# A written-out instruction order, its first part put in another order

## The chip, the cores and the metric

The kernel runs on one core of a Trainium2 chip. The metric is the device time of one execution in microseconds (us). The core has five engines with an instruction stream each: PE (matmuls, into the eight banks of PSUM), ACT (activations, copies out of PSUM, and it can issue DMAs), DVE (vector work), POOL (vector work without PSUM) and SP (which only issues DMAs here). Each stream is executed in its own order; between streams there are semaphores.

## The reference

A transformer block: layer norm, attention with a compressive memory, residual, layer norm, a feed-forward layer with SiLU, residual. 2048 tokens, width 640, 32 heads of 20, four segments of 512 tokens, feed-forward width 1728, bf16.

```python
for s in range(N):                      # N = 4 segments of L = 512 tokens
    logits = einsum(qs, ks) * scale + mask
    p = softmax(logits); a_dot = einsum(p, vs)
    pq = phi(qs)                        # phi(t) = t + 1 if t > 0 else exp(t)
    a_mem = einsum(pq, M) / (einsum(pq, z) + 1e-06)
    outs.append(g * a_mem + (1.0 - g) * a_dot)
    pk = phi(ks)
    M = M + einsum(pk, vs); z = z + einsum(pk)
h = x + concat(outs) @ wo
out = h + silu(layernorm(h) @ w1) @ w2
```

## The kernel before

The work is written as some 1430 tasks with a name each. Functions declare them segment by segment: `declare_front` (layer norm, q and k projections, V, gather copies), `declare_memory`, `declare_ticks` (attention of one group of four heads) and `declare_back` (output projection, second layer norm, feed-forward layer, output). A long string, `ORDER`, then says in which order the tasks are emitted; a word in it is `name/engine:slots`, so `vt05/S:0` is the task `vt05`, issued by SP (A is ACT, D is DVE, G is POOL), with slot 0 of the rotating buffer that it is the first to use. `schedule` reads the words in turn, checks that producers stand ahead and that a slot is free, and appends each task's instructions to the stream of its engine. So the string alone sets each engine's order, the engine of a task that may run on two, and the PSUM banks; there is no timing in it. A `Tracker` adds the semaphore waits that the order needs: a task that writes a PSUM bank waits for the instruction that last read it.

```python
t = todo.pop(name)
t.eng = {"A": AC, "D": DV, "G": PO, "S": SP}[eng] if eng else list(t.engs)[0]
for a in t.allocs:
    if a.slot is None:
        a.slot = slots.pop(0)
```

The tasks of segment 0 that matter here, with their lines and names in `ORDER`:

- projections of q and k by halves of 256 tokens (L867, `pr...x`, `pr...y`) and their evictions from PSUM to SBUF on ACT (L883) or DVE (L884), `qe...`; segment 1 has them whole, 512 tokens wide. `re_wq`, `re_wk` rearrange the weights for them (L693 on ACT, L695 on DVE).
- gather copies (L915, `vt0...`): twelve DMAs that bring rows of q and k of heads 20 to 31 into a layout of their own. They read QK and write QKV; in segment 0 both lie inside the tensor of w2, so that they read w_sb<-w_sb in the trace. The scores of the second four head groups wait for all twelve.
- V projections (L828, `v00` to `v03`, segment 1 `v10` to `v13`), 128 tokens each, and their evictions (L842 on ACT, L843 on DVE, `ve...`).
- scores (L965, `qk...`): four heads at once into four PSUM banks. Then the exp on ACT (L977, `e...`), over two banks (1024 columns) or four (2048), and the causal mask on POOL (L988, `mk...`).
- exponentials of q and k for phi (L890 on ACT, `ex...`), finished on DVE (L897, L903, `pha`, `phb`).
- transposes by DMA: of the normalized tokens of segment 1 (L799, `n1_tr`), of the attention output (L1265, `ot`), of phi(K) (L1208, `kt`). The output projection follows (L1273, `wo0`, `wo1`).
- the feed-forward layer: tanh on ACT (L1317, `th...`), and loads of w1 and w2 (L582, `w_w1_...`, `w_w2_...`). `zf0` and `lsc0` are small exponentials of beta (L649, L638).

Of the kernel before, what the change touches and what calls it, by code (L numbers as in the profile page):

```python
# [324 lines left out]
D = 640  # L325
# [31 lines left out]
epsg0:0 vpad0 zpad w2z/G:0 fill30:7 x0:0 w_q1:0 warm iota mt mta mtb mm7 x1:4 mm0 n1_st1/A:0,0 w_q0 w_q2 epsc sel  # L357
halfc n1_st0/D:5 n1_r0/G n1_r1/D n1_ap0:0 n1_tp0:4 n1_te0a/A:0 n1_ap1:1 n1_tp1:0 n1_te0b/A n1_te1b/D n1_te1a/A w_k0
re_wq1/D:0 pr010x:4 re_wq4/A re_wq2/D pr020x:2 qe020x/A:0 qe010x/A:0 re_wq3/D re_wq0/D pr000x:5 pr040x:6 w_k1
re_wk2/A:0 qe000x/A:0 re_wk1/D qe040x/A:0 pr011x:0 qe011x/A re_wk0/D pr001x:2 pr021x:5 qe001x/A qe021x/A x2:10,5  # L360
n1_st2/D:3 n1_r2/G qk0x10:0 pr030x:7 w_wv0:0 w_wv1 n1_st3/D:1 n1_r3/G e0x10:4 x4:2,1,11,3 qe030x/A:0 w_wo:0 beta
w_w1_0:0 e0x12 re_wk3/D pr031x:6 n1_ap2:2 re_wk4/D x8/S:6,7,8,9 n1_ap3:0 n1_tp2:0 n1_te2/D n1_st6:4 n1_tp3:4 n1_r6/G
n1_te3/A qe031x/D pr041x:7 qe041x/D qk0x20:0 e0x2+:6 pr030y:4 qe030y/D pr031y:5 qe031y/A pr041y:6 qe041y/A pr040y:7
qe040y/A vt02/S:0 vt011/S vt05/S vt08/S n1_st5:1 qk0x30:0 vt04/S mk0x1_0 mk0x1_256 n1_st4:5 n1_r5/G n1_ap5:1 e0x3+:0
n1_ap6:2 pr000y:4 qe000y/D lsc0 vt07/A pr021y:6 qe021y/D pr001y:5 qe001y/D pr011y:7 ex021:0 qe011y/D pr020y:1 n1_r4/D
# [12 lines left out]
h1_0_7_0:6 e6ya+:0 th0_7_0:0 s0_7_0:0 h1_0_12_0:0 th0_12_0:1 qk7ya0:1 e7ya+:1 kt01:0 w_w2_5 h1_0_4_0:7 tn2y:5 s0_12_0
h1_0_3_0:6 kg01/G mk4y1_256 n1_st10:1 th0_3_0:0 mk4y1_384 qvz h1_0_6_0:0 qk4y20:1 th0_4_0:1 nm2y:3 s0_4_0 mm4
h1_0_5_0:5 e4y2+:3 s0_3_0 pr110:7 qe110/D:0 th0_5_0:1 qk4y30:1 pr140:6 th0_6_0:0 e4y32:6 mk4y2_0 e4y30 w_w2_1/S  # L380
mk4y2_256 s0_6_0 s0_5_0 mk4y3_0 mk4y3_256 qe140/D av4y:0 kt03:1 kg03/D ex120:1 qk8a0:4 e8a0:2 e8a2 pr111:1 h1_0_1_0:2
th0_1_0:1 oe4y/D:0 h1_0_8_0:3 th0_8_0:0 qe111/D vt10/S:0 qk8e0:4 s0_1_0 n1_ap8:3 e8e0:4 s0_8_0 mz01:0 ma01/D:3,1
mk4y3_384 av6y:1 e8e2 zf1 qk8b0:2 e8b+:5 kh03/D oe6y/D:1 h1_0_10_0:0 th0_10_0:0 tn4y:6 mzc6 n1_ap9:0 mk8e_0 nm4y:2
tn6y:7 kt04:1 mk8a_0 phb120 nm6y:0 ex100:2 pr130:1 qe130/D:0 qk9a0:3 e9a+:0 s0_10_0 kg04/D pr131:2 qe131/D mk8b_0
pha131:0 h1_0_2_0:7 w_w2_2/S kh04/D th0_2_0:1 mm5 h1_0_11_0:1 th0_11_0:0 s0_11_0 qk9b0:2 e9b0:1 s0_2_0 h1_0_0_0:0
mz02:6 pha101:1 vt13/S mk8b_384 th0_0_0:0 e9b2 mk9a_0 mk9b_0 mk8e_256 h1_0_9_0:7 th0_9_0:1 s0_0_0 ma02/D:0,4,6,7
qk10a0:0 e10a0:3 mzc2 h1_0_13_0:6 h2_0_0:4 e10a2 w_w2_4 ot3 h2_0_1 mk9b_384 mk10a_0 phb101 n1_r10/D pha111:2 vt19/S
mzc0 mb00:0,0 w_w2_3/S s0_9_0 n1_ap11:2 pha100:0 phb100 th0_13_0:0 s0_13_0 ex131:0 phb131 pha110:0 n1_ap10:1 vt12/S
qk10b0:0 e10b+:6 epsg1 av8:7 oe8/D:0 n1_tr8:0 av9:6 oe9/D:1 n1_tr9 ex110:0 phb110 vt18/S vt110/S h2_0_2 mk10b_0
# [1037 lines left out]
```

## Time and profile before

| | |
|---|---|
| three runs | 296.9, 296.9 and 297.67 us, median 296.9 |
| span of the profiled execution | 296.3 us, 0.6 below the median |
| granted PE clock | 1.000 in every stage |
| busy over the span | PE 95%, DVE 75%, ACT 73%, POOL 47% |

The runs are not matched one by one to the profile; the profiled execution's own time is its span and what lies around it, and the 0.6 us between the span and the median is read as that. A timeline row gives start, duration, engine (ACTq and SPq are DMA issues of these engines), line, operation, output and input, and a count where neighbours of one kind are merged; in square brackets stands the idle time before it and what ended that. Consecutive ACT instructions overlap by about 0.1 us in the trace.

### The profile page before, as it was taken

What the parts mean: (1) busy time and instruction counts of PE and PEld (TensorE: products, weight loads), DVE (VectorE), ACT (ScalarE), POOL (GpSimd) and SP (SyncE); (2) the same over time, 40 slices, a digit from 0 to 9 for tenths busy, and PEclk for the clock granted to TensorE, in tenths of its full rate; (3) what the DMA queues carried; (4) which work ended last, traced back from release to release, by engine and by line L of the source; (5) the groups of instructions that cost most, each with busy time, mean ns of one, the idle gap of its engine ahead of it and who ended that gap; (6) DMA issues with size and microseconds to landing.
All of it is one profiled execution on the core that took longest, in us unless ns stands there. A gap on an engine that the chain in (4) does not pass through costs nothing.

```text
span 296.3 us, 7415 instructions
## 1 busy us (share of the span) xinstructions
PE 282.1 (95%) x2968; PEld 167.6 (57%) x2991; DVE 222.2 (75%) x506; ACT 217.3 (73%) x266; POOL 140.0 (47%) x257
## 2 busy tenths in 40 slices
PE   7897889999999999999999999999999999999997
PEld 5675445555665455566643545465665457764575
DVE  3897799778979779899698967759967688626522
ACT  4884989999999899998879999788759750014400
POOL 6237735645566477646526646455476620200000
PEclk9999999999999999999999999999999999999999
DMA  7956973803953221255433400144171023220002
GB/s 243 367 173 105 173 133 71 221 18 75 189 94 74 53 60 22 40 109 106 104 96 61 66 1 2 27 76 87 22 99 32 0 61 74 68 67 25 22 22 91
DMA packets 49922, 25.40 MB, mean 86 GB/s; under 512 B 39504, under 2 KB 48048, under 8 KB 49888
## 3 DMA queue, kind: packets, MB, share of 16 engines
q1 hardware_dynamic: 47804, 22.69, 36.2%
q10 hardware_dynamic: 2084, 2.23, 2.4%
q8 instruction: 24, 0.39, 0.5%
q14 instruction: 10, 0.08, 0.1%
HBM read 10.41 MB, written 2.62 MB: 44 GB/s over the span
## 4 chain that ended last, share of the span: by engine, by line
PE 78%; DVE 8%; DMA 6%; issue 2%; ACT 2%; SPq 1%; POOL 1%; DVEq 0%; ACTq 0%
PE ps_all L1350 19%; PE ps_all L1308 17%; PE ps_all L867 12%; PE ps_all L965 7%; PE ps_all L1273 6%; PE ps_all L828 5%; PE ps_all L1009 5%; DMA x_tok<-in_A_x_dram 3%; DMA xT<-xn_rot 2%; ACT PT L977 2%; PE ps_all L1039 1%; DVE stt L743 1%; PE ps_all L1093 1%; DMA w_sb<-w_sb 1%; PE ps_all L1226 1%
## 5 line engine op out<-in xcount | busy, mean ns | idle before, releaser
L977 ACT ACTIVATE PT<-ps_all 128x1024 bf16<-128x1024 f32 (+1 forms) x120 | 153.2, 1310 | 16.9 <-PE ps_all L965 15.7
L988 POOL TENSOR_SCALAR_AFFINE_SELECT PT<-PT 128x512 bf16<-128x512 bf16 x128 | 81.6, 648 | 59.2 <-ACT PT L977 56.9
L1350 PE MATMUL ps_all<-w_sb,sT 128*128 128x320 bf16 (+2 forms) x462 | 64.9, 295 | 0.0
L1308 PE MATMUL ps_all<-hT,w_sb 128*128 128x512 bf16 (+1 forms) x315 | 61.0, 336 | 1.2 <-issue 0.6
L1317 ACT ACTIVATE th<-ps_all 128x512 f32<-128x512 f32 (+2 forms) x70 | 34.1, 505 | 35.3 <-PE ps_all L1308 31.2
L1350 PEld LDWEIGHTS ps_all<-w_sb,sT 128*128 128x128 bf16 x462 | 43.2, 98 | 18.3 <-issue 1.8
L1323 DVE SCALAR_TENSOR_TENSOR sT<-th,ps_all 128x512 bf16<-128x512 f32 (+2 forms) x70 | 37.9, 561 | 17.8 <-ACT th L1317 16.9
L1308 PEld LDWEIGHTS ps_all<-hT,w_sb 128*128 128x128 bf16 x325 | 29.9, 98 | 25.3 <-issue 3.5
L764 POOL TENSOR_TENSOR rst<-rst,eps_c 128x1 f32<-128x1 f32 x32 | 18.3, 576 | 24.4 <-DVE rst L758 23.1
L743 DVE BATCH_NORM_STATS2 stt<-x_tok 128x6 f32<-128x320 bf16 x62 | 27.2, 481 | 1.1 <-DMA x_tok<-in_A_x_dram 0.7
L1363 DVE SCALAR_TENSOR_TENSOR x_tok<-ps_all,x_tok 128x640 bf16<-128x640 f32 (+3 forms) x18 | 13.3, 745 | 16.7 <-PE ps_all L1350 16.6
L1071 POOL TENSOR_TENSOR otok<-on 128x320 bf16<-128x320 bf16 x24 | 19.0, 797 | 11.7 <-DVE on L1063 11.7
L1273 PE MATMUL ps_all<-wo_sb,oT 128*128 128x320 bf16 x160 | 23.8, 299 | 0.0
L884 DVE CAST QK<-ps_all 128x512 bf16<-128x512 f32 x23 | 15.7, 688 | 9.1 <-PE ps_all L867 8.9
L1063 DVE TENSOR_TENSOR on<-ps_all,rd 128x640 bf16<-128x640 f32 x24 | 19.8, 824 | 0.9
L828 PE MATMUL ps_all<-wv_sb,xT 128*128 128x320 bf16 x120 | 18.3, 299 | 1.1 <-DMA xT<-xn_rot 0.9
L1273 PEld LDWEIGHTS ps_all<-wo_sb,oT 128*128 128x128 bf16 x160 | 15.0, 98 | 7.2 <-issue 1.8
L867 PE MATMUL ps_all<-xT,wkr 128*128 128x512 bf16 x67 | 16.9, 379 | 1.2 <-issue 0.8
L867 PE MATMUL ps_all<-xT,wqr 128*128 128x512 bf16 x70 | 17.3, 380 | 0.4 <-issue 0.2
L1009 PE MATMUL ps_all<-PT,Vx 128*32 128x512 bf16 (+3 forms) x384 | 16.4, 301 | 0.1
L843 DVE CAST Vx<-ps_all 128x640 bf16<-128x640 f32 x15 | 12.3, 818 | 5.4 <-PE ps_all L828 5.3
L770 DVE TENSOR_SCALAR xn_rot<-x_tok,mvt,rst 128x640 bf16<-128x640 bf16 x32 | 14.9, 475 | 1.7 <-POOL rst L764 1.0
(106 smaller groups left out, 337.4 us busy)
## 6 DMA issues: line engine op xcount, KB each, us to landing
w_sb<-in_B_w_dram SPq DMA_DIRECT2D x5, 432.0 KB, 6.3
w_sb<-in_B_w_dram SPq DMA_DIRECT2D x3, 480.0 KB, 4.6
x_tok<-in_A_x_dram SPq DMA_DIRECT2D x2, 640.0 KB, 9.7
out_dram<-x_tok ACTq DMA_DIRECT2D x8, 160.0 KB, 1.8
out_dram<-x_tok SPq DMA_DIRECT2D x7, 160.0 KB, 1.9
x_tok<-in_A_x_dram SPq DMA_DIRECT2D x3, 320.0 KB, 3.4
QKV<-QK SPq DMA_DIRECT2D x12, 72.0 KB
wo_sb<-in_A_wo_dram SPq DMA_DIRECT2D x1, 800.0 KB, 10.4
```

What stands on the lines that cost most here:

```text
L743: T.add(DV, lambda e, hh=hh: e.bn_stats(out=stt[:, s, 6 * hh:6 * hh + 6], in_=xb[:, 320 * hh:320 * hh + 320]), reads=R((xa, xsub)), writes ...
L828: fns.append(lambda e, c=c, hh=hh: e.matmul(bank(ps, hh)[:, 0:320], lhsT=xT_[:, c, 128 * i:128 * i + 128], rhs=wv_sb[:, c, 320 * hh:320 * ...
L867: fns = [lambda e, kc=kc: e.matmul(bank(ps)[:, lo:hi], lhsT=wt[:, kc, c, :], rhs=xT_[:, kc, lo:hi], start=(kc == 0), stop=(kc == NC - 1)) ...
L965: fns.append(lambda e, j=j, o=o, r=r, q0=q0, q1=q1, qa=qa, ka=ka: e.matmul(ps_all[:, o:o + q1 - q0], lhsT=ka[32 * r:32 * r + DH, 128 * j:1 ...
L977: T.add(AC, lambda e: e.activation(out=pt[:, pta.slot, q0:q0 + nq, 0:width], in_=sc3[:, b0:b0 + nq, 0:width], func=ACT.Exp, scale=SCALE), ...
L988: T.add(PO, lambda e: e.affine_select(out=v, in_=v, pattern=[[0, 4], [1, 128]], compare_op=ALU.is_ge, fill=0.0, base=0, channel_multiplier ...
L1009: fns.append(lambda e, j=j, r=r, h=h, pa=pa, pt=pt, co=co, q0=q0, ji=ji: e.matmul(bank(po)[32 * r:32 * r + 32, q0:hi], lhsT=Vx[:, vx.slot, ...
L1273: fns.append(lambda e, c=c, hh=hh: e.matmul(bank(ps, hh)[:, 0:320], lhsT=oT[:, c, 128 * i:128 * i + 128], rhs=wo_sb[:, c, 320 * hh:320 * h ...
L1308: fns = [lambda e, c=c: e.matmul(bank(ps)[:, lo:hi], lhsT=w1_sb[:, c, 128 * f:128 * f + 128], rhs=hT[:, c, lo:hi], start=(c == 0), stop=(c ...
L1317: T.add(AC, lambda e: e.activation(out=th[:, tha.slot, lo:hi], in_=bank(ps)[:, lo:hi], func=ACT.Tanh, scale=0.5), reads=R((ps, [0])), writ ...
L1323: T.add(DV, lambda e: e.scalar_tensor_tensor(out=sT[:, f, lo:hi], in0=th[:, tha.slot, lo:hi], scalar=1.0, in1=bank(ps)[:, lo:hi], op0=ALU. ...
L1350: fns.append(lambda e, f=f, t0=t0, fr=fr, hh=hh, n=n: e.matmul(bank(pa, hh)[:, 0:n], lhsT=sT[:, f, t0:t0 + 128], rhs=w2_sb[:, fr, c0 + 320 ...
```

## The change

Only `ORDER` changes. Of the 1426 words no task is added or removed. Up to about word 447 of 1426 the order, the engines of 28 tasks and the slots are new; after that the sequence of names is the old one, with other numbers for some rotating buffers. Two lines of the diff:

```diff
-re_wq1/D:0 pr010x:4 re_wq4/A re_wq2/D pr020x:2 qe020x/A:0 qe010x/A:0 re_wq3/D re_wq0/D pr000x:5 pr040x:6 w_k1
+w_k1 x2:0,1 re_wq4/A:0 re_wq1/D pr010x:7 qe010x/A:0 re_wq0/D re_wq3/D re_wq2/D re_wk1/A:0 re_wk0/D pr000x:1 pr040x:2
...
```

On ACT the place is between the last four-bank exp of the first score groups and the first one of the second (19 to 29 us before). L977 are exps, L915 gather copies, L890 exponentials for phi, L883 evictions of projections, L842 a V eviction, L638 the small exponential. Before:

```order
L977 ACTIVATE PT<-ps_all 128x2048
L638 ACTIVATE bsel<-beta_bc 128x32
L915 DMA w2_sb<-w2_sb 8x2x1024
L890 ACTIVATE ex<-w2_sb 128x512
L915 DMA w2_sb<-w2_sb 8x2x1024
L915 DMA w2_sb<-w2_sb 12x3x1024 x2
L890 ACTIVATE ex<-w2_sb 128x512
L977 ACTIVATE PT<-ps_all 128x1024 x2
```

After:

```order
L977 ACTIVATE PT<-ps_all 128x2048
L915 DMA w2_sb<-w2_sb 8x2x1024 x2
L883 ACTIVATE w2_sb<-ps_all 128x256 x2
L890 ACTIVATE ex<-w2_sb 128x512
L883 ACTIVATE w2_sb<-ps_all 128x256
L915 DMA w2_sb<-w2_sb 8x1x1024
L883 ACTIVATE w2_sb<-ps_all 128x256
L915 DMA w2_sb<-w2_sb 12x3x1024 x2
L890 ACTIVATE ex<-w2_sb 128x512
L915 DMA w2_sb<-w2_sb 8x2x1024
L977 ACTIVATE PT<-ps_all 128x1024
L842 ACTIVATE Vx<-ps_all 128x32x20
```

ACT now issues six gather copies, four of them behind or between evictions that came from DVE, and it also evicts one V block.

On PE the place is the same stretch: V projections (L828) and scores (L965, twelve matmuls in two rows for a group of three blocks, eight for a group of two). Before:

```order
L828 MATMUL ps_all<-wv_sb,hT 128x320 x20
L965 MATMUL ps_all<-w2_sb 128x256 x4
L965 MATMUL ps_all<-w2_sb 128x128 x8
L828 MATMUL ps_all<-wv_sb,hT 128x320 x10
L965 MATMUL ps_all<-w2_sb 128x256 x4
L965 MATMUL ps_all<-w2_sb 128x128 x8
L828 MATMUL ps_all<-wv_sb,hT 128x320 x10
```

After:

```order
L828 MATMUL ps_all<-wv_sb,hT 128x320 x20
L965 MATMUL ps_all<-w2_sb 128x256 x4
L965 MATMUL ps_all<-w2_sb 128x128 x8
L828 MATMUL ps_all<-wv_sb,hT 128x320 x20
L965 MATMUL ps_all<-w2_sb 128x256 x4
L965 MATMUL ps_all<-w2_sb 128x128 x8
L965 MATMUL ps_all<-w2_sb 128x256 x8
```

The fourth V projection now stands ahead of the first scores that need the gather copies, and the next score group directly behind those.

On ACT again, the stretch from the first tanh instructions (L1317) to the exp from which ACT's order is the old one (58 to 66 us before). Before:

```order
L1317 ACTIVATE th<-ps_all 128x256 x2
L977 ACTIVATE PT<-ps_all 128x2048
L1317 ACTIVATE th<-ps_all 128x256 x2
L977 ACTIVATE PT<-ps_all 128x1024 x2
L890 ACTIVATE ex<-QK 128x512
```

After:

```order
L1317 ACTIVATE th<-ps_all 128x256 x2
L977 ACTIVATE PT<-ps_all 128x2048
L1317 ACTIVATE th<-ps_all 128x256 x2
L649 ACTIVATE zf<-beta_bc 128x32
L977 ACTIVATE PT<-ps_all 128x1024
L582 DMA w2_sb<-in_B_w2_dram 128x3x640
L977 ACTIVATE PT<-ps_all 128x1024
L890 ACTIVATE ex<-QK 128x512 x2
L582 DMA w2_sb<-in_B_w2_dram 128x4x640
```

The small exponential, one exponential for phi and two loads of w2 (SP's before) now stand here.

On SP two transposes of phi(K) (`kt00`, `kt02`) and the w1 load `w_w1_2` move from ahead of the transposes of the attention output to behind them; the load `w_w1_1` moves to behind the last transpose of segment 1's tokens (`n1_tr7`), and `w_w1_3` alone is still ahead of it. On PE the output projections `wo1` and `wo0` move from between the score groups `qk3ya` and `qk4ya` to behind `qk4ya` and ahead of `qk3ya`, and the products for the memory (L1226, `mz00`) from their place at 37 us to one at about 54 us of the old timeline.

More of the change, by code (lines that the diff above doesn't have):

```diff
@@ L361 @@
[L361 to L365, printed above, removed]
@@ new lines @@
+vt10/S:0 kg01/G mz01:0 ma01/D:1,2 qk8e0:4 s0_1_0 mm2 e8e0:5 s0_8_0 mk4y3_384 mm6 av6y:1 n1_ap8:3 e8e2 n1_r9/G zf1
+qk8b0:2 e8b+:4 oe6y/D:1 h1_0_10_0:0 tn4y:6 th0_10_0:0 mzc6 n1_ap9:2 mk8e_0 nm4y:0 tn6y:7 kt04:1 mk8a_0 phb120 nm6y:3
+qvz ex100:0 pr130:1 qe130/D:0 qk9a0:3 e9a+:6 s0_10_0 kg04/D pr131:2 mm4 qe131/D mk8b_0 kh03/D pha131:2 kg03/D
+h1_0_2_0:7 w_w2_2/S kh04/D th0_2_0:1 mm5 h1_0_11_0:1 th0_11_0:0 s0_11_0 qk9b0:2 e9b0:3 s0_2_0 h1_0_0_0:0 mz02:6
+pha101:0 vt13/S mk8b_384 th0_0_0:0 e9b2 mk9a_0 mk9b_0 mk8e_256 h1_0_9_0:7 th0_9_0:1 s0_0_0 ma02/D:3,5,4,7 qk10a0:0
@@ new lines @@
+h1_0_11_1:5 th0_11_1:1 vt29/S pha231:0 phb231 phb211 e17b0 wo6:6 mk16e_256 s0_13_1 s0_11_1 qk18b0:2 e18b2:5 mk17b_0
+e18b0 mk18b_0 rs6 n2_st6:1 ex220:0 av16:0 oe16/D:1 wo7:6 rs7 n2_r6/D qk17a0:2 wo4:0 vt28/S e17a+:6 h1_0_9_1:7
+th0_9_1:0 ex240:2 kg10/G vt27/S n2_st7:4 mk18b_384 vt21/S mk17b_384 vt211/S h1_0_3_1:6 mk17a_0 rs4 th0_3_1:1 n2_st4:7
+s0_9_1 qk18e0:2 e18e0:0 n2_r4/D wo5:0 s0_3_1 vt23/S h1_0_2_1:7 e18e2 mk18e_0 phb240 rs5 th0_2_1:0 s0_2_1 h1_0_1_1:6
+th0_1_1:1 vt24/S s0_1_1 qk18a0:2 e18a0:2 vt25/S av17:1 oe17/A:0 kt23:0 x12/S h2_2_0:6 h2_2_1 n2_ap6:0 n2_st5:2
@@ new lines @@
+th1_7_0:1 th1_4_0:0 s1_7_0 s1_4_0 qk20a0:0 e20a+:6 out3/S x14/S n1_st12:2 n1_r12/G h1_1_1_0:4 th1_1_0:1 s1_1_0 vp210/S
+h1_1_12_0:7 th1_12_0:0 mk20b_0 n1_st13:4 n1_r13/G mk20b_384 vp28/S qk20e0:0 h1_1_11_0:5 n1_ap12:3 e20e+:2 h1_1_8_0:4
+qk21a0:0 s1_12_0 th1_11_0:1 h1_1_5_0:6 e21a+:0 th1_5_0:0 n1_st15:6 mk21a_0 n1_ap13:1 mk20a_0 s1_11_0 s1_5_0 mk20e_0
+mk20e_256 h1_1_2_0:7 th1_2_0:1 s1_2_0 vp20/S qk22a0:0 e22a0:3 kt20:1 vp211/S kg20/G:0 n1_st14:3 vp26/S th1_8_0:1
+kg23/D n1_r14/D h1_1_6_0:5 th1_6_0:0 vp29/S n1_tr12:0 v30:6 n1_r15/D s1_6_0 e22a2 h1_1_0_0:0 n1_ap14:2 s1_8_0
@@ L448 @@
[L448 to L449 removed]
+h2_8_0:0 s2_5_0 th2_9_0:0 s2_11_0 th2_8_0:1 s2_8_0 out4/A wo12:2 ot14 h2_8_1 s2_9_0 wo14:6 rs12 n2_st12:6 rs14
+n2_r12/D n2_st14:5 ot13 wo13:2 rs13 n2_st13:4 ot15 n2_r13/G wo15:6 n2_r14/D rs15 n2_st15:3 h2_8_2 h2_8_3 h2_9_1 o8
+out8/S n2_ap13:2 n2_tr13:0 h2_11_0:2 n2_r15/G n2_ap15:0 h2_11_1 n2_tr15 n2_ap12:1 h2_10_0:6 h2_11_2 h2_10_1 n2_ap14:3
```

149 lines of the change are left out of this document (68 added, 81 removed).

## Prediction

> **What bounds the kernel now.** I read the page's first part, then the windows by stage, then the timelines of ACT, PE and SP in the first 66 us, since the orders differ only there.
>
> ```profile
> PE 282.1 (95%) x2968; PEld 167.6 (57%) x2991; DVE 222.2 (75%) x506; ACT 217.3 (73%) x266; POOL 140.0 (47%) x257
> ```
>
> Over the span PE is the fullest. The stages say more (columns: PE, PEld, DVE, ACT, POOL busy, clock, DMA):
>
> ```profile
> 20.00:30.00 10.00, 8.50 (x86) 6.19 (x84) 8.22 (x20) 5.40 (x7) 5.69 (x11) 1.00 0.53 93
> 30.00:40.00 10.00, 8.49 (x156) 4.80 (x155) 8.28 (x18) 9.30 (x10) 8.10 (x14) 1.00 1.05 181
> 40.00:50.00 10.00, 8.99 (x112) 5.33 (x113) 9.57 (x26) 8.77 (x10) 4.47 (x10) 1.00 0.35 84
> 50.00:56.40 6.40, 5.99 (x87) 2.91 (x82) 5.49 (x14) 6.32 (x9) 3.00 (x5) 1.00 0.79 189
> 56.40:66.00 9.60, 9.10 (x111) 5.33 (x112) 6.83 (x18) 9.56 (x13) 5.35 (x9) 1.00 0.25 66
> 66.00:80.00 14.00, 13.47 (x178) 8.58 (x180) 12.23 (x33) 13.85 (x21) 7.38 (x14) 1.00 0.65 126
> 80.00:90.00 10.00, 10.00 (x119) 6.05 (x118) 8.08 (x20) 9.51 (x10) 6.85 (x15) 1.00 0.55 101
> ```
>
> From 50 to 80 us ACT is busy 29.7 of 30.0 us: scores on PE wait for a PSUM bank that an exp on ACT has to empty, so ACT sets the pace there and PE has 0.5 us of idle time in each 10. Between 20 and 50 us neither engine is full; these holes are what an order can win. From 80 us PE is full. On ACT the two lists are the same from this exp on, on PE from a little later:
>
> ```profile
> 66.03 1.94 ACT L977 ACTIVATE PT<-ps_all 128x1024 bf16<-128x1024 f32 x2
> ```
>
> The waits from there on are the same too, but for a few on work that is long done. So the change can only shift the instant at which ACT and PE enter the common part; that shift is the forecast. I follow ACT from mark to mark:
>
> ```profile
> 18.28 0.93 ACT L883 ACTIVATE w_sb<-ps_all 128x256 bf16<-128x256 f32 x3
> 19.12 1.88 ACT L977 ACTIVATE PT<-ps_all 128x2048 bf16<-128x2048 f32 x1
> 19.24 1.62 ACTq L915 DMA_DIRECT2D w_sb<-w_sb  x1
> ...
> 21.36 0.63 ACT L890 ACTIVATE ex<-w_sb 128x512 bf16<-128x512 bf16 x1 [0.24 <-DVE w_sb L884]
> 21.36 3.34 ACTq L915 DMA_DIRECT2D w_sb<-w_sb  x3
> 24.75 0.63 ACT L890 ACTIVATE ex<-w_sb 128x512 bf16<-128x512 bf16 x1 [2.76 <-DVE Vx L843]
> 25.56 1.94 ACT L977 ACTIVATE PT<-ps_all 128x1024 bf16<-128x1024 f32 x2 [0.18 <-PE ps_all L965]
> 28.92 1.88 ACT L977 ACTIVATE PT<-ps_all 128x2048 bf16<-128x2048 f32 x1 [1.43 <-PE ps_all L965]
> 31.30 1.88 ACT L977 ACTIVATE PT<-ps_all 128x2048 bf16<-128x2048 f32 x1 [0.50 <-PE ps_all L965]
> 33.07 0.62 ACT L890 ACTIVATE ex<-w_sb 128x512 bf16<-128x512 bf16 x1
> 33.68 3.71 ACT L977 ACTIVATE PT<-ps_all 128x1024 bf16<-128x1024 f32 x3
> ```
>
> ```profile
> 28.47 0.40 PE L965 MATMUL ps_all<-w_sb 20*128 20x256 bf16 x12 [1.50 <-DMA w_sb<-w_sb]
> 28.80 1.53 PE L828 MATMUL ps_all<-wv_sb,hT 128*128 128x320 bf16 x10
> ...
> 37.00 0.48 PE L1226 MATMUL ps_all<-Vx,phiKt 128*128 128x84 bf16 x8
> ...
> 42.68 1.53 PE L828 MATMUL ps_all<-wv_sb,xT 128*128 128x320 bf16 x10 [0.85 <-DMA xT<-xn_rot]
> 44.48 2.89 PE L1273 MATMUL ps_all<-wo_sb,oT 128*128 128x320 bf16 x20
> ```
>
> Mark A is ACT's exp at 28.92: it follows the scores at 28.47, for which PE stood 1.50 us until the twelve gather copies (L915) had landed. Mark B is 33.68.
>
> **The change part by part.** Up to 18.28 us projections and weight rearrangements trade places, and one rearrangement of wk goes from DVE to ACT.
>
> ```profile
> 10.01 0.66 ACT L883 ACTIVATE w_sb<-ps_all 128x256 bf16<-128x256 f32 x2 [0.72 <-PE ps_all L867]
> 10.56 0.83 ACT L693 ACTIVATE wkr<-sT 128x400 bf16<-128x400 bf16 x2
> ```
>
> One more costs ACT 0.83; the hole of 0.72 covers most of it, and one eviction (0.31) goes the other way while another comes. I take 0.1 us later at the exp that ends the stretch; ends 0 and 0.8 (the hole not used).
>
> *Gather copies, to mark A.* SP issued eight and ACT four; now it is six and six.
>
> ```profile
> 19.23 6.07 SPq L915 DMA_DIRECT2D w_sb<-w_sb  x8
> 25.34 1.31 SPq L799 DMA_TRANSPOSE xT<-xn_rot  x1
> ...
> 30.81 0.90 SPq L582 DMA_DIRECT2D w_sb<-in_B_w_dram  x1
> ...
> 33.02 1.05 SPq L582 DMA_DIRECT2D w_sb<-in_B_w_dram  x2
> 35.73 1.21 SPq L799 DMA_TRANSPOSE xT<-xn_rot  x1
> ```
>
> One issue takes 6.07/8 = 0.76 us. On ACT it is hidden while an instruction given out before it still runs: the first, at 19.24, lies under the exp 19.12 to 21.00. It is not hidden otherwise: from 21.36 on, three issues and one exponential filled 3.4 us. In the new order two copies stand right behind the exp of the third score group (hidden), one beside an eviction (half hidden), two after an eviction that they wait for (not hidden, 1.52), one beside an exponential (nearly hidden). From the exp's start at 19.7 (an eviction and an exponential now stand ahead of it: +0.6): 1.8 for the exp, 0.6 two evictions (0.31 each), 0.6 exponential, 0.3 eviction, 0.4 for the half-hidden issue, 0.4 eviction, 1.5 two issues, 0.75 for exponential and last issue, end 26.1. The last issue before ended at 25.30 and the scores began at 28.47, 3.2 later; but those copies shared the queue with the transpose of 25.34, and the last one now goes out on ACT's own. I take 2.6 to 3.2: landed between 28.7 and 29.3. ACT meanwhile runs an exp of two banks (0.97), a V eviction new on ACT, and the second exp (0.97). No row has this eviction on ACT; the 128x512 one (0.60, quoted below) and a 128x1024 exp (0.97) bound it, I take 0.75. So ACT is free at 26.1 + 0.97 + 0.75 + 0.97 + 0.1 = 28.9. PE no longer stands: the fourth V projection (1.53) now fills the wait. Mark A: 29.0, +0.1; ends -0.5 (all hidden, landing at 28.0) and +2.4 (the four covered issues bare, 3.0, less 0.6 that the landing would hide).
>
> [...]
>
> *A to B.* Of the 4.76 us, 0.50 was idle, waiting for scores behind a V projection, and 0.52 an exponential. The exponential now stands before A and the scores' banks are free in time. But the scores of B reuse banks that the exp before has to empty, so ACT waits some 0.5 for them. B: -0.4 with the 0.1 from A; ends 0 and -0.9.
>
> *B to C, the exp at 47.75.*
>
> ```profile
> 44.59 1.02 ACT L977 ACTIVATE PT<-ps_all 128x1024 bf16<-128x1024 f32 x1 [0.84 <-PE ps_all L965]
> ...
> 47.75 1.94 ACT L977 ACTIVATE PT<-ps_all 128x1024 bf16<-128x1024 f32 x2 [0.18 <-PE ps_all L965]
> 49.57 0.60 ACT L883 ACTIVATE QK<-ps_all 128x512 bf16<-128x512 f32 x1
> 50.15 1.88 ACT L977 ACTIVATE PT<-ps_all 128x2048 bf16<-128x2048 f32 x1
> 51.92 0.22 ACT L649 ACTIVATE zf<-beta_bc 128x32 f32<-128x32 bf16 x1
> 52.04 0.62 ACT L890 ACTIVATE ex<-QK 128x512 bf16<-128x512 bf16 x1
> 52.74 5.54 ACT L977 ACTIVATE PT<-ps_all 128x1024 bf16<-128x1024 f32 x5
> ```
>
> The 0.85 at 42.68 was a V projection waiting for a transpose issued at 35.73, behind three weight loads (0.90 and 1.05 us of issue). Two of the loads and two transposes of phi(K) now stand behind it, so that it should be there in time; the 0.84 of ACT at 44.59 goes with it. New is that both output projections (2.89) now stand between two score groups: ACT finishes the group before and waits. From B at 33.3: 3.7 three exps, 0.55 exponential, 1.9, 0.1, 1.9, 1.9 exps, 0.5 exponential, 1.9 exps: 45.8. PE starts the output projections at 43.7, is through at 46.6, the next scores take 0.40: exp at 47.0, which is -0.7 against C. Ends -1.3 (projections half a us early) and 0 (their transposes late).
>
> *C to the common part.* 1.9 + 0.5 + 1.9 + an eviction of 0.6 that was DVE's: 52.0 against 52.74, still -0.7. Then ACT has what stood at 51.92 and 52.04 still to do, in a stretch with 0.04 us of room in 9.60: +0.1 and +0.52. Two loads of w2 now issued by ACT stand right behind running instructions of 1.0 and 0.6: hidden by the row of 19.24, ends 0 and 1.0 (0.6 and 0.4, bare). The products for the memory (0.48 at 37.00) moved here; PE has 0.41 + 0.50 idle from 50 to 66: 0, ends 0 and 0.4. Sum at 66.03: -0.7 + 0.6 = -0.1.
>
> *Elsewhere:* the evictions that change engine between ACT and DVE are in the sums above where they are on ACT; Four phi steps of DVE move into 56.4 to 66, each at most as long as this one:
>
> ```profile
> 51.75 0.42 DVE L903 TENSOR_TENSOR phiK<-phiK,ex 128x512 bf16<-128x512 bf16 x1
> ```
>
> That is 1.7 at most, and DVE has 9.60 - 6.83 = 2.8 idle there; were that cover gone, evictions of QK and the scores behind them would be late by as much. POOL (4.2 idle) covers the layer-norm steps and masks that it gets.
>
> Sum: the profiled execution spans 296.3, 0.6 below the median of the runs, 296.9; I take the 0.6 as lying around it. 296.9 - 0.1 and a tenth of idle time that ACT loses in 66 to 80 (0.15 there): **296.7**.
>
> **Rivals.** *Slower: the gather copies land late.* If the issues on ACT aren't covered, or SP and ACT wait for one another while issuing (the 1.62 of the first against 0.76 speaks for that; the row of 19.24 as a whole speaks against bare issues), A slips by up to 2.4, and ACT passes it on, being full behind. It decides at A = 30.1: then the 0.2 won turns into 0.9 lost. Half the price, +1.2, gives 298.1; all of it 299.1.
>
> *Faster: the payment at the end is smaller or the start better.* If copies land at 28.2 and ACT's two late instructions cost 0.2 for 0.6, the shift is -0.1 - 0.7 - 0.4 = -1.2: 295.7. For it: PE's holes of 1.50 and 0.85 both go. Against it: ACT has no room after 50 us.
>
> *Kept half:* the projections' place at C costs nothing or everything, -0.6 to +0.7 around the forecast: 296.1 to 297.4, both within 0.3%.
>
> **How the numbers follow.** 0.3% (0.9 us) is about what a measurement can tell from no change. Forecast with its neighbours within 0.9 us: 0.46. Faster by more: 0.30, mostly 295.0 to 296.0. Slower by more: 0.24, mostly 297.9 to 299. Range 295.2 to 298.4: it leaves out a tenth on either side. Within the likeliest case alone 296.0 to 297.7.
>
> **What the next profile would show.** Right: PE's wait of 1.50 for w_sb<-w_sb gone, a V projection in its place; mark A within 0.5 of 28.9; no wait of 0.85 for xT; an idle of about 1.2 on ACT before the exp after the output projections; ACT full from 52 to 66 and the exp of 66.03 within 0.5. Wrong: A at 30 or later, or a wait on DVE's evictions near 63 to 66.

## The result, and the profile after

The changed kernel takes 301.47 us (median of four runs, 299.95 to 302.58) against 296.9: ratio 1.0141, 95% interval 1.0101 to 1.0181. By the ratio it is slower by 4.2 us, by the medians by 4.6, and it lies 3.1 us above the upper end of the predicted range. The profiled execution is the fastest of the four: span 298.1, its own time 299.95. In these four runs and in every run since, the time is the span plus 1.7 to 1.9. So the 0.6 that the prediction laid "around the span" was wrong: the execution of before that it read (span 296.3) must have taken about 298.1, some 1.2 above its kernel's median.

First the page's busy line and the line of the granted clock, after:

```profile
PE 286.4 (96%) x2991; PEld 168.8 (57%) x2991; DVE 219.5 (74%) x499; ACT 219.4 (74%) x272; POOL 140.4 (47%) x258
```

```profile
core 0: 298.1 us, clock 0.994
```

PE's 4.3 us more of busy time are no gain: 23 more matmuls are in the records (the order has the same), and matmuls at half clock count nearly double (ten matmuls of a V projection that take 1.53 us take 2.87 in c1 below). The windows by stage, after (columns as before), show where:

```profile
20.00:30.00 10.00, 8.32 (x90) 5.77 (x87) 7.37 (x20) 5.88 (x12) 6.82 (x13) 1.00 0.68 103
30.00:40.00 10.00, 7.91 (x128) 4.35 (x120) 5.61 (x11) 8.15 (x7) 5.19 (x9) 0.83 0.25 60
40.00:50.00 10.00, 8.79 (x93) 4.96 (x85) 7.87 (x19) 8.66 (x9) 3.32 (x6) 1.00 0.57 136
50.00:56.40 6.40, 6.30 (x94) 3.09 (x93) 5.51 (x15) 6.17 (x8) 3.66 (x7) 1.00 0.51 143
56.40:66.00 9.60, 9.02 (x116) 5.56 (x117) 6.66 (x16) 9.56 (x13) 3.09 (x5) 1.00 0.18 38
```

Between 30 and 40 us the mean clock is 0.83, ACT is busy for 8.15 instead of 9.30 us, and DVE for 5.61 instead of 8.28. The timeline of PE there, after:

```profile
25.81 2.04 PE L828 MATMUL ps_all<-wv_sb,hT 128*128 128x320 bf16 x13
29.53 0.62 PE L965 MATMUL ps_all<-w_sb 20*128 20x256 bf16 x20 [1.68 <-DMA w_sb<-w_sb]
31.91 0.52 PE L1093 MATMUL ps_all<-PT,Vx 128*32 128x256 bf16 x16 [1.76 <-ACT PT L977]
32.36 2.52 PE L828 MATMUL ps_all<-wv_sb,xT 128*128 128x320 bf16 x10
34.81 0.61 PE L965 MATMUL ps_all<-w_sb 20*128 20x256 bf16 x12
```

PE stands twice (the row at 29.53 and the row at 31.91). The first stand is for the gather copies, although the fourth V projection now lies ahead. Then both score groups are issued at once and fill all eight PSUM banks, so the next matmul (L1093, probabilities times V) finds no free bank until the first exp has emptied four; c1 below shows that it is the banks. Behind that, a V projection takes 2.52 us instead of 1.53: the clock has gone to half. The windows of 3.41 us around it (the column before the last two is the clock):

```profile
25.91:29.32 3.41, 1.94 (x14) 1.00 (x12) 2.87 (x7) 1.98 (x4) 1.36 (x4) 1.00 1.13 127
29.32:32.73 3.41, 1.44 (x39) 0.95 (x40) 0.42 (x3) 2.75 (x2) 1.40 (x4) 1.00 0.69 178
32.73:36.15 3.42, 3.42 (x37) 1.79 (x39) 1.93 (x4) 1.57 (x2) 2.49 (x4) 0.50 0.01 2
```

ACT, after, with its issues:

```profile
22.68 1.66 ACTq L915 DMA_DIRECT2D w_sb<-w_sb  x2
24.38 0.63 ACT L890 ACTIVATE ex<-w_sb 128x512 bf16<-128x512 bf16 x1 [1.73 <-issue]
24.40 0.79 ACTq L915 DMA_DIRECT2D w_sb<-w_sb  x1
...
27.65 0.24 ACT L638 ACTIVATE bsel<-beta_bc 128x32 f32<-128x32 bf16 x1
29.98 3.65 ACT L977 ACTIVATE PT<-ps_all 128x2048 bf16<-128x2048 f32 x2 [2.09 <-PE ps_all L965]
35.48 3.71 ACT L977 ACTIVATE PT<-ps_all 128x1024 bf16<-128x1024 f32 x3 [1.85 <-PE ps_all L965]
...
49.21 1.94 ACT L977 ACTIVATE PT<-ps_all 128x1024 bf16<-128x1024 f32 x2 [1.22 <-PE ps_all L965]
...
67.04 1.18 ACT L890 ACTIVATE ex<-QK 128x512 bf16<-128x512 bf16 x2
68.08 1.97 ACT L977 ACTIVATE PT<-ps_all 128x1024 bf16<-128x1024 f32 x2
```

Mark A is 29.98, B 35.48, C 49.21, and the exp that begins the common part 68.08. From there to the end the distance to the kernel before stays between 1.9 and 2.2 us. But the executions did not begin alike: the exp of the third score group of segment 0 starts at

```profile
16.50 1.88 ACT L977 ACTIVATE PT<-ps_all 128x2048 bf16<-128x2048 f32 x1 [0.19 <-PE ps_all L965]
```

before, and at 15.91 after. Below, "S+" counts from this exp (S), and marks are S+:

| kernel, profiled execution | A | B | C | exp of 52.74 before | exp of 66.03 before |
|---|---|---|---|---|---|
| before | 12.42 | 17.18 | 31.25 | 36.24 | 49.53 |
| predicted | 12.5 | 16.8 | 30.5 | 35.5 | 49.4 |
| after | 14.07 | 19.57 | 33.30 | 38.29 | 52.17 |
| c2 (below): copies in time, clock kept | 12.36 | 16.66 | 30.39 | 35.38 | 49.25 |

### The profile page after: what moved, and what is told of

Read it like the earlier page. It is cut to its first block, busy times and chain, and to the rows that moved or that the text cites. A ratio compares the mean times of both kernels' runs of the same rounds, so it can differ in the third digit from the quotient of the medians.

```text
span 298.1 us, 7440 instructions
## 1 busy us (share of the span) xinstructions
PE 286.4 (96%) x2991; PEld 168.8 (57%) x2991; DVE 219.5 (74%) x499; ACT 219.4 (74%) x272; POOL 140.4 (47%) x258
## 4 chain that ended last, share of the span: by engine, by line
PE 79%; ACT 9%; DVE 4%; DMA 3%; issue 1%; ACTq 1%; POOL 1%; DVEq 0%
PE ps_all L1350 19%; PE ps_all L1308 17%; PE ps_all L867 12%; ACT PT L977 8%; PE ps_all L965 7%; PE ps_all L1273 7%; PE ps_all L828 5%; PE ps_all L1009 5%; DMA w_sb<-w_sb 2%; PE ps_all L1039 1%; ACTq L915 1%; PE ps_all L1226 1%; PE ps_all L1043 1%; DMA x_tok<-in_A_x_dram 1%; PE ps_all L1302 1%
## 5 line engine op out<-in xcount | busy, mean ns | idle before, releaser
L977 ACT ACTIVATE PT<-ps_all 128x1024 bf16<-128x1024 f32 (+1 forms) x120 | 153.1, 1311 | 18.9 <-PE ps_all L965 17.4
L1308 PE MATMUL ps_all<-hT,w_sb 128*128 128x512 bf16 (+1 forms) x325 | 62.7, 337 | 0.1
L1317 ACT ACTIVATE th<-ps_all 128x512 f32<-128x512 f32 (+2 forms) x70 | 33.9, 505 | 35.3 <-PE ps_all L1308 31.3
L884 DVE CAST QK<-ps_all 128x512 bf16<-128x512 f32 x22 | 15.1, 687 | 6.8 <-PE ps_all L867 6.6
L828 PE MATMUL ps_all<-wv_sb,xT 128*128 128x320 bf16 x120 | 19.3, 310 | 0.5 <-ACT PT L977 0.2
L867 PE MATMUL ps_all<-xT,wkr 128*128 128x512 bf16 x75 | 18.7, 380 | 0.0
L867 PE MATMUL ps_all<-xT,wqr 128*128 128x512 bf16 x75 | 18.2, 380 | 0.0
L1281 DVE TENSOR_TENSOR x_tok<-ps_all,x_tok 128x640 bf16<-128x640 f32 x16 | 12.9, 809 | 4.0 <-PE ps_all L1273 4.0
L843 DVE CAST Vx<-ps_all 128x640 bf16<-128x640 f32 x14 | 11.5, 821 | 5.8 <-PE ps_all L828 5.8
```

Of the source, the lines that this page charges most:

```text
L828: fns.append(lambda e, c=c, hh=hh: e.matmul(bank(ps, hh)[:, 0:320], lhsT=xT_[:, c, 128 * i:128 * i + 128], rhs=wv_sb[:, c, 320 * hh:320 * ...
L867: fns = [lambda e, kc=kc: e.matmul(bank(ps)[:, lo:hi], lhsT=wt[:, kc, c, :], rhs=xT_[:, kc, lo:hi], start=(kc == 0), stop=(kc == NC - 1)) ...
L977: T.add(AC, lambda e: e.activation(out=pt[:, pta.slot, q0:q0 + nq, 0:width], in_=sc3[:, b0:b0 + nq, 0:width], func=ACT.Exp, scale=SCALE), ...
L1308: fns = [lambda e, c=c: e.matmul(bank(ps)[:, lo:hi], lhsT=w1_sb[:, c, 128 * f:128 * f + 128], rhs=hT[:, c, lo:hi], start=(c == 0), stop=(c ...
L1317: T.add(AC, lambda e: e.activation(out=th[:, tha.slot, lo:hi], in_=bank(ps)[:, lo:hi], func=ACT.Tanh, scale=0.5), reads=R((ps, [0])), writ ...
```

## Experiments

Theory: the last gather copies land late because a transpose is issued on SP's queue at the same moment; PE then stands for them, and once more for want of a bank; the clock falls to half for one window; ACT hands the delay on. SP's queue there, after, against the last copy's issue on ACT at 24.40 above:

```profile
24.53 3.51 SPq L799 DMA_TRANSPOSE xT<-xn_rot  x2
```

Rivals: the banks alone, the clock alone, or the price paid later, from C on. All edits are words of the order string; `fillN` is a task of the kernel's own, N idle matmuls of 128x256. Every kernel is compared with runs of the kernel before on the same chip (medians 296.96 to 297.34).

**Stands filled.** `fill13` ahead of both score groups (a1), of the second alone (a3), of the first alone (c4):

```diff
-... vt00/S qk4x10:0 lsc1 vpad1 lsc2 qk4x20:4 ...
+... vt00/S fill13:7 qk4x10:0 lsc1 vpad1 lsc2 fill13:7 qk4x20:4 ...
```

> The changed order with 13 idle-filling matmuls (128x256, nothing reads them) in each of the two stretches in which PE stood: ahead of the scores that wait for the gather copies, and between the two score groups behind them. No other word moves. Theory clock: the loss behind the gather copies comes from the granted clock, which fell to 0.50 for 3.4 us after PE had stood 1.68 and 1.76 us; with PE kept busy it stays 1.000, the V projection that took 2.45 us takes 1.5, and the run is 1.0 to 1.5 us faster than the changed kernel. Theory waits: the late landing and the PSUM banks cost what was lost and the clock nothing, since ACT sets the pace: within 0.3 us of the changed kernel.

> The changed order with 13 idle-filling matmuls in the second stretch alone, between the two score groups behind the gather copies. Theory clock: the second stretch lies in the 3.4 us before the fall, so it alone decides: clock 1.000 and the same gain as with both, 1.0 to 1.5 us. If both stretches count together, half the runs or none keep the clock. Theory waits: no change within 0.3 us.

> The changed kernel with 13 idle matmuls (128x256, into a free bank) ahead of the first score group only: the stand of 1.7 us for the copies is filled, the stand of 1.8 us behind the second score group remains. Theory (the clock falls because both stands come within some 4 us, PE working under half of the time): with one of the two gone it is kept in all runs; time 299.6 as with both filled (299.63), at most 0.4 off. Rival (a single stand of 1.8 us is enough): clock 0.994 in half of the runs or more, time 300.6 or more, as with only the second stand filled (300.64).

a1: 299.63 us, ratio 1.0086 (1.0070 to 1.0103), clock 1.000 in all four runs. That is 1.8 us below the changed kernel (1.6 by the ratios), an estimate of what the clock costs. PE, a1:

```profile
28.00 1.59 PE L620 MATMUL ps_all<-zpad 128*128 128x256 bf16 x13
30.25 0.40 PE L965 MATMUL ps_all<-w_sb 20*128 20x256 bf16 x12 [0.65 <-issue]
30.58 1.59 PE L620 MATMUL ps_all<-zpad 128*128 128x256 bf16 x13
```

The copies came even later here (the last of them landed at 30.16, S+14.1, against S+13.4 after), and the time fell all the same. One fill does little or nothing: a3 300.64 (1.0093 to 1.0157) and c4 301.62 (1.0098 to 1.0177). The clock lost a window in one run of a3's four (a second one shows 0.999) and in two of c4's. Both were to keep the clock, and c4 to reach 299.6: both missed. A single stand is enough in part of the runs, and their copies landed 5.2 and 5.0 us after their issue.

**Banks.** The first group's scores stay in banks 0 to 3, `av0x` and `v11` go ahead of the second group, which waits for banks 0 to 3 as in the kernel before (c1):

```diff
-... qk4x10:0 lsc1 vpad1 lsc2 qk4x20:4 e4x1+:2 pha001:2 av0x:2 n1_tr5:0 v11:0 lsc3 oe0x/D:0 n1_tr6 ...
+... qk4x10:0 lsc1 vpad1 lsc2 lsc3 e4x1+:2 pha001:2 av0x:5 n1_tr5:0 v11:6 oe0x/D:0 ve11/D:1 qk4x20:0 n1_tr6 ...
```

> The changed kernel with other PSUM banks behind its first score group: scores of the first group in banks 0 to 3 as now, av0x in bank 5, the V projection v11 in 6 and 7, both ahead of the second score group, which goes back to banks 0 to 3 (as the kernel before had both groups in the same banks); the third group's scores in 4 to 7; the evictions oe0x and ve11 directly behind their matmuls. Nothing is left out. Theory (three steps: copies land late, then the banks are all taken, then the clock falls): the first step stays (first exp at 29.4 to 30.7), the second is taken away: PE works through av0x and v11 while that exp runs, the second exp starts 0.4 to 0.6 later than in the changed kernel, the third at about 34.3 instead of 35.48, and the clock is kept at 1.000 in most runs. Time about 299.6 (298.9 to 300.3), 1.8 below the changed kernel. Rival (the banks do not matter, PE stood only because it had nothing to do in any order): the second exp is late by 0.5 and nothing comes back, 301.5 to 302.

303.01 us, 1.0145 to 1.0255: against the theory. PE, c1, and its windows:

```profile
30.08 0.40 PE L965 MATMUL ps_all<-w_sb 20*128 20x256 bf16 x12 [2.03 <-DMA w_sb<-w_sb]
30.41 0.52 PE L1093 MATMUL ps_all<-PT,Vx 128*32 128x256 bf16 x16
30.86 2.18 PE L828 MATMUL ps_all<-wv_sb,xT 128*128 128x320 bf16 x10
```

```profile
28.18:31.59 3.41, 1.51 (x34) 1.09 (x35) 2.07 (x5) 1.06 (x1) 1.99 (x5) 1.00 0.93 185
31.59:35.01 3.42, 2.60 (x26) 0.94 (x24) 1.30 (x3) 2.19 (x2) 2.11 (x3) 0.50 0.32 64
35.01:38.42 3.41, 2.65 (x47) 1.38 (x48) 2.12 (x4) 3.09 (x4) 2.21 (x4) 0.50 0.00 0
38.42:41.83 3.41, 3.41 (x22) 1.63 (x21) 1.72 (x4) 1.63 (x2) 0.96 (x2) 0.50 0.54 83
```

The second stand is gone as intended (the row at 30.41 follows the scores at once), yet the stand for the copies alone leaves 1.51 us of work in one window, and the clock stays at half for three. So the banks make the stand of 1.76, but they are not what decides.

**Copies earlier, or the transposes later.** a2 issues the last copy, `vt04`, right behind `vt07` on ACT; c2 moves three normalizations on DVE behind `ve03`, so that SP's transposes start at 28.32 instead of 24.53; c3 is a2 with the banks of c1; b1 goes the other way, on the kernel before (its last copy behind the transpose `n1_tr5` on SP):

```diff
 a2:  vt07/A +vt04/A vt02/S ... vt06/A ... ex021:1 -vt04/A qk0y10:4
 c2:  -n1_ap5:0 ... -n1_ap6:2 ... -n1_ap4:1 ... ve03/D +n1_ap5:0 +n1_ap6:2 +n1_ap4:1 ve02/D
 b1 (before): +n1_tr5 ahead of vt01/S, -n1_tr5 behind it
```

> The changed order, with one gather copy (the last that landed) moved on ACT from behind the second exponential to right behind the first two copies, under the four-bank exp. Theory landing: the copies land at 28.0 to 28.4 instead of 29.3 and everything behind is 0.9 to 1.3 us earlier; if the clock then stays up too, 2.0 to 2.5. Theory queue: SP and ACT wait for one another while issuing, so that the moved copy delays the others as much: within 0.3 us of the changed kernel.

> The changed kernel with the normalizations n1_ap5, n1_ap6 and n1_ap4 moved on VectorE behind the eviction ve03, so that SP issues the token transposes n1_tr5, n1_tr6 and n1_tr4 some 3 us later (from about 27.8 instead of 24.53); the twelve gather copies keep their queues and order. Theory (the transpose's 256-byte packets hold the last copy's packets back): the last copy lands about 3 us after its issue ends, at 28.0 to 28.5 instead of 29.3 to 30.4, and the first exp starts at 28.6 to 29.2; time 298.0 to 300.0 (299.0; as with the copy issued early, 299.01). Rival (the last copy is late because four copies follow each other on ACT's queue, whatever SP issues): it lands at 29.2 to 30.4 all the same, first exp about 30, time 301 to 302.

> Both repairs together: the last copy vt04 issued early on ACT (directly behind vt07), and the banks of c1_banks. Theory: landing 28.2, first exp 28.8, PE works through av0x and v11 while it runs (stands of together 1.6 us on PE gone but for about 0.3), second exp at about 31.2, third at about 33.1, clock 1.000 in all runs, PE gains up to 1 us on the way to the first FFN work (e0y3+ at 48.3 to 49.2 against 49.18). Time 297.4 (296.4 to 298.3), level with the kernel before (297.05 median of its runs so far). Rival (with the copies in time the rest of the loss lies elsewhere in the new order): 298.4 or more, as the runs of the kernel with the copy early that kept the clock.

> The kernel before with one transpose (1.3 us of SP's issuing) put ahead of the last gather copy. The copies land 1.3 us later and PE stands 2.8 us instead of 1.5. Theory clock: a longer stand drops the clock in the old order too: 1.3 us of wait and another 1 us or so behind it, 2.0 to 2.6 slower than before, clock 0.994. Theory waits: 1.0 to 1.4 slower at clock 1.000. Theory slack: nothing, because ACT catches up: within 0.4 of before.

a2: 299.01 (1.0038 to 1.0083). c2: 299.61 (1.0038 to 1.0091); of its ten runs three kept the clock, 296.91 to 297.97, and seven did not, 299.09 to 301.91. With the copies in time and the clock kept, then, the new order is within 1 us of the kernel before (297.01 on that chip). SP's transposes, PE's scores (no wait for the copies) and ACT's exp in c2:

```profile
28.32 2.63 SPq L799 DMA_TRANSPOSE xT<-xn_rot  x2
```

```profile
28.51 0.40 PE L965 MATMUL ps_all<-w_sb 20*128 20x256 bf16 x12
```

```profile
28.96 3.65 ACT L977 ACTIVATE PT<-ps_all 128x2048 bf16<-128x2048 f32 x2 [0.40 <-PE ps_all L965]
```

The time from the end of the last copy's issue to the last landing (the last semaphore count of the twelve copies in the trace) tells the theory from its rival.

| last copy's issue to last landing | us |
|---|---|
| on ACT, a transpose issued on SP beside it | 4.1 (after), 4.8 (a1), 5.2 (a3), 4.4 (c1), 5.0 (c4) |
| the same copies in the same order, transposes later | 2.4 (c2, and d1 below), 2.5 (d3 below) |
| `vt04` early, transposes as after | 3.1 (a2), 3.6 (c3) |
| `vt04` early, transposes later | 2.95 (d2 below) |
| old order: on SP, the transpose behind it on the same queue | 3.0 (before), 3.3 (e0, its second profile), 2.95 (e2 below) |
| old order, transposes 2 us later | 2.6 (d4 and e1 below) |
| old order, the copy behind the transpose | 2.1 (b1) |

So the small copy on ACT's queue lands 1.7 to 2.8 us later with a transpose issued on SP's beside it; the last copy on SP's own queue lands only 0.4 to 0.7 later with the transpose behind it. What in the transfers does that is not shown. With `vt04` early the last copies are other, larger ones, and their time says little of the transpose.

c3, 299.82 (1.0061 to 1.0120), missed: the banks gave nothing with early copies either. b1, 298.76 (1.0025 to 1.0068), lost mostly by the clock: 299.19 on average in five runs with a fall, 297.68 in four without. Its copies came 0.5 later (S+12.3 against S+11.8), not the 1.3 foreseen.

**Both repairs, and a third cause.** d1 is c2 with `fill11` ahead of the second score group; d2 adds the early `vt04` and moves `zf0` and `ex101` away from the exp of 66.03, ahead of which the prediction had them cost 0.62; d3 is d1 with the copy `kg02` behind three other steps on DVE:

```diff
 d1:  lsc2 +fill11:7 qk4x20:4
 d3:  kt02:1 -kg02/D n2_st0:2 w_w1_4 ... n2_r0/G n2_ap0:0 +kg02/D n2_r1/G
```

> The transposes late as in c2_tr_late, and 11 idle matmuls (128x256, into a free bank) ahead of the second score group, where PE stood 0.88 us and then another 0.70 us behind it. Theory (two causes and no third: the last copy held up by the transpose's packets, and the clock that falls when PE is busy for less than about 0.45 of a 3.41 us window): both are gone, so the clock stays at 1.000 in nearly every run and the time is that of the runs of c2_tr_late that kept the clock, 297.5 (296.7 to 298.2), within 0.3% of the kernel before (297.01). Rival (the new order loses something else that only some runs show): clock 1.000, but 298.5 or more.

> As d1_late_fill, and besides: the copy vt04 issued early on ACT (behind vt07), zf0 on ACT moved into its idle time behind e4ya2, and ex101 behind e8a2. Nothing is left out. Theory: the copies land at about 27.6 instead of 28.3 and the first exp starts as soon as v02 and the scores are through, 0.3 to 0.5 earlier; zf0 and ex101 take 0.8 us of ACT out of the way of e8a0, of which PE's score group leaves 0.2. Time 296.9 (296.2 to 297.5), with the clock at 1.000: level with the kernel before or up to 0.2% below it. Rival (the lower bound is set elsewhere, by PE before e8a0 or behind it): 297.5 as d1_late_fill.

> As d1_late_fill, with the copy kg02 on VectorE moved behind the two normalization statistics n2_st0 and n2_st1 and behind n2_ap0, so that the landing of the transposing transfer kt02 (1.3 us after its issue in some profiles, 2.6 to 3.1 in others) no longer holds VectorE. Theory (a third cause: the change moved kt02's issue from 26.80 to 46.13, 3 us before its use): the step from e5ya2 to e6ya+ is 3.63 us in the profile instead of 4.52, the runs lose their upper half, and the median falls from 298.5 to 297.7 (297.2 to 298.1), clock 1.000. Rival (the spread of the runs comes from elsewhere, the landing of the gather copies above all): median 298.2 to 298.6, spread as in d1_late_fill.

d1: clock 1.000 in all twelve runs, as foreseen, but 298.52 (1.0017 to 1.0055) instead of 297.5. Its profile has a wait on DVE:

```profile
47.70 0.21 DVE L1199 COPY phiKv<-phiKt 128x192 bf16<-128x192 bf16 x1 [0.59 <-DMA phiKt<-phiK]
```

In the kernel before, the transposes of phi(K) were issued from 26.80 on and used at 48.97 on POOL; the change issues them here, after:

```profile
44.82 2.58 SPq L1208 DMA_TRANSPOSE phiKt<-phiK  x2
```

The second lands 1.3 us after its issue in five profiles of the new order and 2.4 to 3.1 in six others (a1, a3, c4, d1, d2, d3). In the first five of these it held DVE by 0.3 to 0.8, and so the layer norm behind it, an eviction and the third exp from mark 52.74 on; from that mark to the fifth exp (56.37 before) it is 4.52 us in d1, 4.44 to 4.76 in the five, and 3.63 both before and after. With `kg02` moved (d3) DVE stands no more and the step is 3.73 (3.63 was expected): 297.83, all eight runs at clock 1.000, 1.0019 to 1.0050. The step in the trace is shown; its worth in the runs is not. The medians of d1 and d3 differ by 0.7, but d3 ran on another chip, against the kernel before on the same chip the two ratios are alike (1.0036 and 1.0035), and the runs overlap (297.17 to 299.66 and 297.18 to 298.79). d2, 299.05 (1.0035 to 1.0076), missed: its copies landed no earlier, `kt02` held DVE for 0.80, and what `zf0` and `ex101` gave before the exp of 66.03 (0.23) was lost again by the last exp (0.23).

**The same causes in the old order.** d4 issues the transposes of the kernel before 2 us later (`n1_ap5` behind `phb001` on DVE); e2 moves three weight loads behind `n1_tr7` on SP; e1 does both; e0 is the kernel before, profiled again.

> The kernel before with one instruction moved: the normalization n1_ap5 goes on VectorE behind phb001, so that SP issues the transposes n1_tr5, kt02 and n1_tr6 some 2 us later, behind the gather copies. Theory (transposes that are issued beside the copies delay the copies): the last copy lands 2.4 us after its issue ends instead of 3.0, the first exp of the second score groups starts 0.4 to 0.6 earlier, and the time falls to 296.6 (296.2 to 297.0) against 297.05. Rival (in the old order the last copy and the transposes are on the same queue, and what is behind a copy there does not delay it): landing 3.0 after issue, time 296.9 to 297.3; or the later transposes come late for the V projections: 297.5 or more.

> The kernel before, unchanged, for a second profile. The profiled execution shown with the case took 1.1 us more than the median, and its first second-group exp lay 12.42 us behind the exp e0x2+, as in no other profile of the old order can be checked. Theory (its start was late by 0.6, the rest was typical): e0x2+ at 15.9 to 16.1, first exp of the second score groups at 28.2 to 28.5, e8a0 at 65.3 to 65.6, span 294.8 to 295.6. Rival (the start is late in every run, the difference lies behind the marks): e0x2+ at 16.5 again.

> d4_before_tr_late mended: the normalization n1_ap5 behind phb001 as there, and the three weight loads w_w1_2, w_w1_3 and w_w1_1 on SP moved behind the transpose n1_tr7, which in d4 landed 5.6 us after its issue and kept the V projection v13 waiting for 1.99 us. Theory: the copies land 2.6 us after their last issue (first exp 0.42 earlier against e0x2+, as in d4), n1_tr7 lands within 3 us, v13 waits no longer, the clock stays at 1.000: 296.2 (295.6 to 296.8), below both kernels. Rival (the time is set elsewhere once these waits are gone, by ACT and PE from 44 us on): 296.8 to 297.2.

> The kernel before with only the three weight loads w_w1_2, w_w1_3 and w_w1_1 moved behind n1_tr7 on SP. Theory (loads that stand ahead of a transpose on its queue delay its landing): n1_tr7 lands within 3 us of its issue instead of 5.7, the wait of 0.85 us on PE at 42.68 goes, and with it ACT's 0.84 before e3ya0; 296.4 (296.0 to 297.0). Rival (the transpose is slow whatever stands ahead): the wait stays, 297.0.

d4 moved A from S+12.42 to S+12.00, with the landing 2.6 after issue (2.4 expected). But it was to take 296.6 and took 298.9 (1.0050 to 1.0088). In its profile `n1_tr7` lands 5.6 after its issue, behind the same weight loads, and a V projection stands for it; the clock falls behind that. The runs without a fall took 298.4 to 299.06 all the same:

```profile
42.86 2.07 PE L828 MATMUL ps_all<-wv_sb,xT 128*128 128x320 bf16 x10 [1.99 <-DMA xT<-xn_rot]
```

e2: `n1_tr7` lands 2.9 us after its issue instead of 5.7, and the 0.85 is gone, but the time is 297.61 (1.0000 to 1.0045) where 296.4 was expected: no gain. e1, expected at 296.2, took 298.09 (1.0019 to 1.0047); there the first V projection of segment 1 waits 0.70 for its transpose. e0 bears on that. It began at S = 15.87, it lost a clock window (298.47 us), and it has no 0.85 either: its `n1_tr7` landed 2.4 after the issue, behind the same three loads. In the four profiles that have the loads ahead of `n1_tr7`, it lands 5.7 (before), 5.6 (d4), 2.3 (b1) and 2.4 us (e0) after its issue. So the wait that the prediction counted on winning belongs to some executions only; in how many is not known, and that e2 gained nothing speaks for few. No version beat the kernel before.

## Why the prediction was wrong, step by step

- *Start to the copies' issue*: right. The issues on ACT under a running exp were free, and the last issue ended at S+9.3 (25.19), against S+9.6 in the sum. The slower rival had nearly the right mark (A at S+14.07; its 30.1 is S+13.6) and a wrong reason, bare issues: ACT was free at 27.89 and stood 2.09 for scores. With the covered issues bare, ACT would have lost the prediction's 2.4 in issuing. The trace after does not bear that out: the exp at 19.00 began under an issue that ran from 18.61 to 20.15.
- *"I take 2.6 to 3.2: landed between 28.7 and 29.3"*: the step that failed. It measured 4.1 (landed at 29.29, S+13.4), in other profiles of these issues up to 5.2. The range came from copies that shared a queue with the transpose; "the last one now goes out on ACT's own" was noted and not priced. That is 1.65 us at A.
- *"PE no longer stands"*: wrong. PE stood 1.68 and 1.76. That the banks are free was looked up for ACT's scores only, where it held (no idle between the two exps), and not for what PE has to do behind them.
- *The clock* has no term in the sum at all. Runs that lost one window took longer than runs of the same kernel that lost none by 1.5 us on average in b1 and by 2.2 in c2; in kernels with only one such run it was 0.7 (e1) to 3.0 (e2). A late landing in the same run may be part of that. It fell in all four runs after.
- *A to B, B to C*: with copies in time and clock kept (c2) they are what was predicted: -0.5 and -0.9 at B and C against -0.4 and -0.7; ACT's idle before C 1.22 against "about 1.2"; the pay-back between 52.74 and 66.03 0.58 against 0.62; the sum at 66.03 -0.28 against -0.1.
- *The transposes of phi(K)*, named as moved, had no price for their own landing: 0 to 1.1 at the fifth exp.
- *The base*: -0.85 was for a wait that not every execution of before has; e2, without it, stands at S+49.11, 0.4 below the profile before. So marks level with that profile (d3, S+49.55) can still mean more time: some 0.4 of the 0.9 us by which d3's median lies above.

An estimate from these: landing 1.7 to 2.8, clock 1.5 to 2.2, phi(K) 0 to 1.1, base 0.4, together 3.6 to 6.5 against 4.2 to 4.6. The terms are not independent, since a late landing also empties the 3.41 us ahead of the fall (1.44 us of work in them after). Open: why the landing beside a transpose spreads from 4.1 to 5.2; why in about half the profiles a transposing issue takes 2.0 to 2.6 us instead of 1.3 (a3, with the latest landing, has none of these); and 0.5 of the 0.9 left in d3.

## What to carry to other kernels

Price a moved DMA by where its neighbours go on the other queues, not by its own issue: a small copy on ACT's queue landed 4.1 to 5.2 us after its issue with a transpose issued on SP's beside it, and 2.4 without. Add up PE's work in each 3.4 us of a stretch with new waits: here two stands, of 1.68 and 1.76 us, left 1.44 us of work in 3.41, and after the stands themselves the clock was lost too, at half for the next 3.41 us. And before a wait of under 1 us in one profile is counted as a gain, look whether a second execution has it.

## What the runs showed of the hardware

The changes of the clock lay whole multiples of 3.413 us apart in the profiles before and after. After, it rose at 5.43, fell to half at 32.73 (8 x 3.413 later), was back at 36.15 and fell again at 298.97, behind the last instruction (86 x 3.413 from the rise). Before, it rose at 3.92 and fell only behind the last instruction, at 297.47, also 86 x 3.413 later. In the six profiles with a fall during the work, the 3.41 us ahead of the first half-clock stretch had PE busy for 1.36 to 1.61 us (a3 1.36, b1 and d4 1.43, after 1.44, c1 1.51, e0 1.61). The clock stayed full behind 1.68 (c4) and 1.89 (c3), and behind every other such stretch, counted from the rise to the end of PE's work, in the profiles after (1.94 or more) and before (2.20 or more). The most that a fall followed and the least that none followed, e0 and c4:

```profile
26.00:29.41 3.41, 1.61 (x22) 0.96 (x21) 3.17 (x7) 1.69 (x2) 2.09 (x5) 1.00 0.74 94
```

```profile
31.97:35.38 3.41, 1.68 (x26) 1.18 (x26) 1.02 (x2) 3.41 (x2) 1.53 (x3) 1.00 0.39 102
```

The clock came back behind 3.41 us of half clock with PE busy throughout (after, a3, b1, d4, e0); in c1 it was still at half behind 2.60 and 2.65 us of work, and back behind 3.41. In the profile after, the 4.00 us from 28.00 to 32.00 held 0.71 us of work (0.47, 0.15 and 0.09) at full clock, and the fall came at 32.73, at the end of the stretch from 29.32. So the author's reading, which no run tests by itself, is that the fall of one order depends on where these stretches begin and on the landing of that execution. In the first profile of the kernel before no 3.41 us between 18 and 51 us hold less than 1.91, wherever they begin; in e0, with the copies 0.3 later, one stretch held 1.61. The kernel before fell in 2 of 88 executions of these comparisons. A fall followed single stands of PE of 1.80 (e0), 1.99 (b1 and d4) and 2.03 us (c1).
